# Transposes on halves of 64 rows and a regrouped attention step in a fused attention and mixture-of-experts kernel

## Chip, cores and metric

The kernel runs on one NeuronCore of a Trainium2 chip. The metric is the time of one execution on the device in microseconds (us); the result before is the median of three runs. An engine executes its own queue in order: TensorE (PE, with its weight loads PEld), VectorE (DVE), ScalarE (ACT), GpSimd (POOL); SyncE (SP) issues most DMAs. Engines wait for one another by semaphores.

## What is computed

Local attention (window 64) over 4 x 8 heads of 576 x 64, then a dense two-layer part with ELU, then eight experts weighted by a normalised gate:

```python
scores = scale * np.matmul(q, k.transpose(0, 1, 3, 2))
mask = (rel >= 0) & (rel < window)
scores = np.where(mask, scores, -1000000000.0)
attn = np.exp(scores - np.max(scores, axis=-1, keepdims=True))
attn = attn / (np.sum(attn, axis=-1, keepdims=True) + 1e-09)
x = np.matmul(attn, v)                 # reshaped to (2304, 512)
h = x @ w_in
g = np.where(h > 0.0, h, alpha * (np.exp(np.minimum(h, 0.0)) - 1.0))
x = g @ w_out                          # (2304, 512) -> 2048 -> 512
logits = x @ w_gate                    # gate, normalised 8 times by rows and columns
for e in range(E):
    out += P[:, e:e + 1] * (np.maximum(x @ w1[e], 0.0) @ w2[e])
```

All arithmetic is float32; products are split into high and low parts (three matmuls of 512 columns each take the place of one).

## The kernel before

The program has an attention loop of 27 steps, the rest of the dense part, and the experts. The change concerns the loop alone. It is written as a hand-made order: each engine executes its instructions in the order in which the Python code issues them.

Heads go in 16 pairs (`pair_load`, q and k of two heads). A pair has 9 chunks of 64 positions, taken in 3 groups; a step of the loop handles two groups, that is 6 chunks of two heads, in a software pipeline. In step m the loop issues

- `pair_T`: PE transposes q and k for step m+1 (four transposes of 96 columns for each of two groups, tile `ptr`), and ACT copies them to `qkT`;
- `step_S`: the scores of step m, 12 matmuls on quarters of the array (the trace shows 24, two passes each), tiles `s`; DVE adds the mask and takes the row minimum of the negated scores in six custom instructions (L368), three for each head, into `sp` and `smx`;
- `grp_E`: six exponentials of step m-1 on ACT (L383), and `step_N`: DVE's reciprocal and POOL's multiplication (L399);
- `grp_P`: PE transposes the weights of step m-2 (six transposes of 128 columns, tiles `pt`), and ACT copies them to `pT`;
- `step_V`: P times V of step m-3, tile `pv` (24 matmuls in the trace); `grp_XH` copies it on ACT to `xh`, and `grp_X` subtracts on DVE, giving the low part `xl` (L454);
- up to three slots (`slot`), each for one product of the dense part: six matmuls of 512 columns. An incoming product (`m0_in`, L473 to L475, "i") is half of a bank `p1`; when the second half is done, `elu` issues relu (L238) and exp (L239) on ACT, max (L227) on DVE, a copy to `gh` (L231) on ACT and a subtraction to `gl` (L235) on DVE. An outgoing product ("o", L491 to L493) ends after two with a DVE copy. A budget of 16/6 a step says how many slots are filled. Where a product is not ready, the first steps issue a warm-up matmul (`warm`);
- background work (`run_bg`): conversion of the 64-bit weights by DVE and ACT (L152 to L163), POOL's split of them (L179, L180), and their loads (`w_load`) on SP; `v_load` and `v_shift` bring v and a copy of it shifted by 64 rows (`ve`).

PSUM has four buffers of the pool tagged `ac` (`ps_ac`) for `s`, `ptr`, `pv` and one `pt`, one tagged `sm` for the other `pt`, and three for products. A tag's buffers are handed out in turn, so a new tile waits for the readers of the one issued four requests ago. A step makes six requests of `ac`: before in the order s, s, ptr, ptr, pv, pt.

The order of PE in a step before is scores, one or two products, q/k transposes, P times V, a product, P's transposes. "Step 15" in the text is the step whose scores are the 15th, counted from 0.

Of the kernel before, what the change touches and what calls it, by code (L numbers as in the profile page):

```python
# [8 lines left out]
F32 = mybir.dt.float32  # L9
# [9 lines left out]
def kernel(  # L19
# [88 lines left out]
    def ps_ac(name):  # L108
        return ps.tile([P, 512], F32, tag="ac", bufs=4, name=name)
# [77 lines left out]
    def run_bg(n):  # L187
        for _ in range(min(n, len(bg))):
            bg.pop(0)()
# [61 lines left out]
        return gh, gl  # L251


    NTQ, TQ = 6, S // 6
    qk_nat, v_nat, qk_T = {}, {}, {}

    def pair_load(pi):
        b, hp = divmod(pi, NPAIR)
        h0 = 2 * hp
        t = {}  # L260
        for z, (nm, src) in enumerate((("q", q), ("k", k))):
            if pi % 3 == 2:
                w = NTQ * 2 * D
                x = acc[3][:TQ, z * w:(z + 1) * w].rearrange("p (t h d) -> p t h d", h=2, d=D)
            else:
                x = at.tile([TQ, NTQ, 2, D], F32, tag="nat", bufs=4, name=f"{nm}n")
            for h in range(2):
                (nc.scalar if pi == 0 and z else nc.sync).dma_start(
                    out=x[:, :, h, :],
                    in_=src[b, h0 + h].rearrange("(t p) d -> p t d", p=TQ),  # L270
                )
            t[nm] = x
        qk_nat[pi] = t

    def v_load(pi):
        b, hp = divmod(pi, NPAIR)
# [28 lines left out]
                    0.0, 1.0, op0=ALU.add, op1=ALU.mult,  # L305
                )

    def pair_T(n):
        pi, g = divmod(n, NG)
        if g == 0:  # L310
            qk_T[pi] = at.tile([P, 2, S], F32, tag="qkT", bufs=2, name="qkT")
        pt = ps_ac("ptr")
        per = NTQ // NG
        for m, nm in enumerate("qk"):
            for t in range(per):
                o = (m * per + t) * TQ
# [5 lines left out]
        w = per * TQ  # L322
        nc.scalar.activation(
            qk_T[pi][:, :, g * w:(g + 1) * w],
            pt[:, :2 * w].rearrange("p (m t) -> p m t", m=2), AF.Copy,
        )

    g_st = {}

# [70 lines left out]
                out=sp, in0=sp, in1=w[:, :, h:h + 1].to_broadcast([P, GRP, P]), op=ALU.mult  # L400
            )

    def grp_P(m, h):
        sp = g_st[m, h]
        pt = (ps_ac if h else ps_sm)("pt")
        for l in range(GRP):
            nc.tensor.transpose(pt[:, P * l:P * l + P], sp[:, l, :], ident)
        pT = at.tile([P, GRP * P], F32, tag="pT", bufs=2, name="pT")
        nc.scalar.activation(pT, pt[:, :GRP * P], AF.Copy)
        g_st[m, h] = pT  # L410

    def step_V(m, pv):
        pTs = [g_st.pop((m, h)) for h in range(2)]
        for x in range(2 * GRP):
            pi, c = at_chunk(2 * GRP * m + x)
            ve, vo = v_nat[pi]
            vt, w = (vo, (c - 1) // 2) if c % 2 else (ve, c // 2)
            for h in range(2):
                nc.tensor.matmul(
                    pv[D * h:D * h + D, WIN * x:WIN * x + WIN],  # L420
                    vt[:, w, h, :],
                    pTs[h][:, WIN * x:WIN * x + WIN],
                    start=True,
                    stop=True,
                )
# [824 lines left out]
    with tc.manual_schedule():  # L1250
# [26 lines left out]
                nc.tensor.matmul(pw, wz[:, 0:P], wz, start=True, stop=True)  # L1277

        warm(8)
        for n in range(2):  # L1280
            pair_T(n)
        for kk in range(2 * UF):
            bg += w_tasks(kk)
        NGRP = B * NPAIR * NG
# [31 lines left out]
        for m in range(NST + 3):  # L1316
# [4 lines left out]
            if m == 0:  # L1321
                w_load(0)
                pair_load(2)
                w_load(1)
            if ready():
                budget += 16.0 / per_b
            rate = (0, 0) if m == 0 else (2, 2) if m < 8 else (6, 2)
            mm, mo, mf = m - 1, m - 2, m - 3
            if mid:
                grp_E(mm, 0)  # L1330
            if new:
                step_S(m)
            slot(m, 2)
            run_bg(rate[0])
            if mid:
                grp_E(mm, 1)
            slot(10, 1)
            if mid:
                step_N(mm)
            for n in nxt:  # L1340
                pair_T(n)
            for n in mid if m == 4 else old:
                if n > NG and n % NG == 0 and (n // NG > 2 or m == 4):
                    v_shift(n // NG)
            if fin:
                pv = ps_ac("pv")
                step_V(mf, pv)
                grp_XH(fin, pv)
            slot(m, 0)
            grp_X()  # L1350
            if old:
                grp_P(mo, 0)
                grp_P(mo, 1)
            if fin and (m - 2) % per_b == 0:
                avail += subs[(m - 2) // per_b - 1]
            if m == 13:
                bg += [w_tasks(2 * UF + x)[0] for x in range(2)]
            run_bg(rate[1])
# [7 lines left out]
        grp_X()  # L1366
        avail += subs[4]
        attn_cm.__exit__(None, None, None)
        wb_cm, wb = pool("wb")
# [225 lines left out]
```

## Time and profile before

| | us |
|---|---|
| median of three runs | 1969.49 (1969.34 to 1969.82) |
| profiled execution | 1974.2 |
| its span | 1972.4 |
| PE busy | 1954.1 (99%) |
| DVE busy | 1494.2 (76%) |
| ACT busy | 858.4 (44%) |
| POOL busy | 726.1 (37%) |

The shares are means over the whole span; the attention loop is the first 173 us of it, and there they differ from stage to stage. Matmuls overlap, so what one costs is read from the distance between starts, and a busy PE can still be waiting inside its pipeline. "Idle before" names what ended a wait, as inferred from semaphores.

### The profile page before, as it was taken

Reading aid. Unit: us, or ns where it says so; the run is one execution under the profiler, and the core shown is the slowest. Engines: PE = TensorE matmul, PEld = TensorE weight load, DVE = VectorE, ACT = ScalarE, POOL = GpSimd, SP = SyncE. Lnnn points to the kernel's source line nnn. Section 1 sums busy time; section 2 is a strip of 40 time slices with the busy share of each in tenths; the row PEclk is TensorE's granted clock in tenths of the full one; section 3 lists DMA queues with packets and bytes.
Section 4 is the critical chain, followed back from the end, with each engine's and each line's share of the span. In section 5 each row is a group of like instructions: output and inputs, shape, how many; then the busy total and the mean of one; then the engine's idle time right before and its main releaser. Section 6 shows DMA issues by size and latency. Waiting matters only on the chain.

```text
span 1972.4 us, 33582 instructions
## 1 busy us (share of the span) xinstructions
PE 1954.1 (99%) x11856; PEld 1816.9 (92%) x11856; DVE 1494.2 (76%) x2534; ACT 858.4 (44%) x1801; POOL 726.1 (37%) x723
## 2 busy tenths in 40 slices
PE   8999999999999999999999999999999999999999
PEld 6788888898878888899999999999999999999998
DVE  6746676767698656567787888888888888888886
ACT  8875555555543444333343333333334333333332
POOL 5423232332355554342342323323343323333232
PEclk9999999999999999999999999999999999999999
DMA  9851354467699999868878888888887887888884
GB/s 212 165 110 52 100 173 151 154 210 275 213 381 374 374 366 365 314 234 284 263 242 305 260 261 257 255 266 262 291 260 250 270 266 259 260 260 262 238 279 121
DMA packets 307640, 487.84 MB, mean 247 GB/s; under 512 B 79872, under 2 KB 161936, under 8 KB 303632
## 3 DMA queue, kind: packets, MB, share of 16 engines
q1 hardware_dynamic: 306288, 485.39, 76.3%
q8 instruction: 95, 1.56, 0.3%
q14 instruction: 73, 0.60, 0.1%
q10 hardware_dynamic: 1184, 0.30, 0.1%
HBM read 354.44 MB, written 126.95 MB: 244 GB/s over the span
## 4 chain that ended last, share of the span: by engine, by line
PE 90%; DVE 4%; DMA 2%; ACT 2%; SPq 1%; issue 1%; POOL 0%; ACTq 0%; DVEq 0%; POOLq 0%
PE la L1080 15%; PE ob L1160 11%; PE oa L1160 11%; PE lb L1080 11%; PE p L204 3%; PE ac L538 3%; PE p L206 3%; PE ac L540 3%; PE p L205 2%; PE ac L539 2%; PE ac L904 2%; PE ac L905 2%; PE ac L906 2%; PE p L886 2%; PE p L888 2%; PE p L887 2%
## 5 line engine op out<-in xcount | busy, mean ns | idle before, releaser
L1062 POOL TENSOR_TENSOR h<-s,h 128x384 fp32r<-128x384 f32 x304 | 352.6, 1175 | 721.1 <-ACT h L1053 680.2
L1080 PE MATMUL la<-xf,w1f 128*128 128x384 f32 x1824 | 360.0, 335 | 1.9 <-ACT u L1100 1.3
L1080 PEld LDWEIGHTS la<-xf,w1f 128*128 128x128 f32 x1824 | 318.3, 188 | 3.4 <-ACT u L1100 2.1
L1080 PE MATMUL lb<-xf,w1f 128*128 128x384 f32 x1368 | 273.7, 334 | 0.0
L1053 ACT ACTIVATE h<-s 128x384 fp32r<-128x384 f32 x304 | 155.1, 522 | 245.7 <-DVE s L1104 238.4
L1160 PE MATMUL oa<-h,w2f 128*128 128x384 f32 x1344 | 252.2, 334 | 0.0
L1160 PE MATMUL ob<-h,w2f 128*128 128x384 f32 x1344 | 252.0, 334 | 0.2 <-DVE acc L1177 0.2
L1080 PEld LDWEIGHTS lb<-xf,w1f 128*128 128x128 f32 x1368 | 239.9, 188 | 0.0
L1160 PEld LDWEIGHTS ob<-h,w2f 128*128 128x128 f32 x1344 | 234.4, 188 | 0.5 <-DVE acc L1177 0.5
L1160 PEld LDWEIGHTS oa<-h,w2f 128*128 128x128 f32 x1344 | 234.4, 188 | 0.1
L1058 DVE SCALAR_TENSOR_TENSOR h<-c,h 128x384 fp32r<-128x384 f32 x228 | 187.6, 833 | 31.9 <-ACT h L1053 31.2
L1053 ACT ACTIVATE h<-c 128x384 fp32r<-128x384 f32 x228 | 119.7, 525 | 173.7 <-DVE c L1090 162.6
L725 POOL TENSOR_TENSOR sw<-rw 128x256 f32<-128x256 f32 x110 | 101.0, 919 | 204.6 <-DVE f L755 127.8
L1090 DVE TENSOR_TENSOR c<-c,pb 128x384 f32<-128x384 f32 x192 | 144.5, 753 | 6.6
L1177 DVE TENSOR_TENSOR acc<-oa,acc 128x768 f32<-128x768 f32 (+1 forms) x114 | 105.0, 924 | 37.4 <-PE oa L1160 37.4
L1177 DVE TENSOR_TENSOR acc<-ob,acc 128x768 f32<-128x768 f32 (+1 forms) x110 | 101.2, 923 | 37.1 <-PE ob L1160 37.1
L1104 DVE SCALAR_TENSOR_TENSOR s<-c,s 128x384 f32<-128x384 f32 x152 | 108.3, 713 | 12.0 <-DMA out_dram<-ost 1.0
L246 ACT ACTIVATE hh<-p 128x512 fp32r<-128x512 f32 (+1 forms) x80 | 39.2, 490 | 171.9 <-PE p L888 171.8
L247 DVE SCALAR_TENSOR_TENSOR hl<-p,hh 128x512 fp32r<-128x512 f32 (+1 forms) x80 | 44.3, 556 | 88.5 <-ACT hh L246 88.5
L886 PE MATMUL p<-xh,f 128*128 128x512 f32 (+1 forms) x320 | 108.4, 339 | 0.0
L887 PE MATMUL p<-xl,f 128*128 128x512 f32 (+1 forms) x320 | 107.6, 336 | 0.0
L888 PE MATMUL p<-xh,f 128*128 128x512 f32 (+1 forms) x320 | 107.5, 336 | 0.0
(175 smaller groups left out, 3907.3 us busy)
## 6 DMA issues: line engine op xcount, KB each, us to landing
w1f<-wdi SPq DMA_DIRECT2D x532, 256.0 KB, 4.0
w2f<-wdo SPq DMA_DIRECT2D x266, 512.0 KB, 4.4
wdo<-f SPq DMA_DIRECT2D x28, 1024.0 KB, 7.7
rw<-in_moe_w_dram SPq DMA_DIRECT2D x220, 128.0 KB, 4.9
wdi<-f SPq DMA_DIRECT2D x27, 1024.0 KB, 7.1
wdo<-f SPq DMA_DIRECT2D x28, 768.0 KB, 5.6
wdi<-f SPq DMA_DIRECT2D x27, 768.0 KB, 5.0
raw<-in_moe_w_in_dram SPq DMA_DIRECT2D x16, 512.0 KB, 4.3
```

The lines of the kernel that those rows point to most:

```text
L725: nc.gpsimd.tensor_tensor(out=sw[:, o], in0=a, in1=b, op=op)
L886: nc.tensor.matmul(p1[:, :n], w[:, s, 0, cs], xh, start=(c == 0), stop=False)
L887: nc.tensor.matmul(p1[:, :n], w[:, s, 0, cs], xl, start=False, stop=False)
L888: nc.tensor.matmul(p1[:, :n], w[:, s, 1, cs], xh, start=False, stop=(c == NCC - 1))
L1053: nc.scalar.activation(h[:, 0], src, AF.Relu if relu else AF.Copy)
L1058: nc.vector.scalar_tensor_tensor(h[:, 1], src, 0.0, r(h[:, 0]), op0=ALU.max, op1=ALU.subtract)
L1062: nc.gpsimd.tensor_tensor(out=h[:, 1], in0=src, in1=r(h[:, 0]), op=ALU.subtract)
L1080: nc.tensor.matmul(o, w[:, a, c, :], x[:, b, c, :], start=first and c == 0 and z == 0, stop=last and c == 1 and z == 2, skip_group_check=True,
L1090: nc.vector.tensor_tensor(out=t, in0=t, in1=pb[g, e][:, i], op=ALU.mult)
L1104: nc.vector.scalar_tensor_tensor(d[nm], d[a], 0.0, d[b], op0=ALU.max, op1=op)
L1160: nc.tensor.matmul(o[:, c], w[:, p, b, c * P:(c + 1) * P], hs[p][:, a, :], start=fresh and p == 0 and z == 0, stop=False, skip_group_check ...
L1177: nc.vector.tensor_tensor(out=a, in0=src, in1=a, op=ALU.add)
```

## The change

Two things change. First, transposes: q and k of a pair now lie in one tile of 128 rows (q in rows 0 to 63, k in rows 64 to 127, nine chunks of 64), and both q/k and P are transposed in halves of 64 rows, which alternate between two PSUM tiles; the two tiles are then copied to SBUF by ACT, one for q (or the upper half) and one for k (or the lower half). Second, the order of a step: P times V of step m-3 with its copies, scores, exponentials, P's transposes, q/k transposes, `v_shift`, conversions, normalisation, and then all slots. A step's requests of `ac` now come as pv, s, s, pt, ptr, ptr. Products of a block can begin in the step whose P times V completes it, since that now stands ahead of the slots.

```diff
-    def pair_T(n):
...
-                nc.tensor.transpose(
-                    pt[:, o:o + TQ],
-                    qk_nat[pi][nm][:, g * per + t].rearrange("p h d -> p (h d)"),
-                    ident[:TQ, :TQ],
-                )
...
+    def step_T(ns):
+        pts = [ps_ac("ptr") for _ in range(2)]
...
+            for b in range(GRP):
+                for z, zs in enumerate(halves):
+                    nc.tensor.transpose(
+                        pts[z][:, o + b * WIN:o + b * WIN + WIN],
+                        qk_nat[pi][zs, g * GRP + b].rearrange("p h d -> p (h d)"),
+                        ident[zs, zs],
+                    )
...
+        for pi, t0, o, w in segs:
+            for z in range(2):
+                nc.scalar.activation(qk_T[pi][:, z, t0:t0 + w], pts[z][:, o:o + w], AF.Copy)
...
-    def grp_P(m, h):
...
-        for l in range(GRP):
-            nc.tensor.transpose(pt[:, P * l:P * l + P], sp[:, l, :], ident)
...
+    def step_P(m):
+        pts = [ps_sm("pt"), ps_ac("pt")]
+        for h in range(2):
+            for l in range(GRP):
+                o = (GRP * h + l) * WIN
+                for z, zs in enumerate(halves):
+                    nc.tensor.transpose(pts[z][:, o:o + WIN], g_st[m, h][zs, l, :], ident[zs, zs])
...
-            if mid:
-                grp_E(mm, 0)
-            if new:
-                step_S(m)
-            slot(m, 2)
-            run_bg(rate[0])
-            if mid:
-                grp_E(mm, 1)
-            slot(10, 1)
-            if mid:
-                step_N(mm)
-            for n in nxt:
-                pair_T(n)
...
             if fin:
                 pv = ps_ac("pv")
                 step_V(mf, pv)
                 grp_XH(fin, pv)
+                grp_X()
+                if (m - 2) % per_b == 0:
+                    avail += subs[(m - 2) // per_b - 1]
+            if ready():
+                budget += 16.0 / per_b
+            if new:
+                step_S(m)
+            if mid:
+                grp_E(mm, 0)
+                grp_E(mm, 1)
+            if old:
+                step_P(mo)
+            if nxt:
+                step_T(nxt)
...
+            run_bg(rate[0])
+            if mid:
+                step_N(mm)
+            slot(m, 2)
+            slot(10, 1)
             slot(m, 0)
-            grp_X()
-            if old:
-                grp_P(mo, 0)
-                grp_P(mo, 1)
-            if fin and (m - 2) % per_b == 0:
-                avail += subs[(m - 2) // per_b - 1]
```

On PE, before, around the scores of step 18 (`p_1976` is a bank of incoming products, `[waits ...]` the engines whose semaphores an instruction waits for):

```order
L473 MATMUL p_1976<-xh_94,w0h 128x512
L474 MATMUL p_1976<-xl_99,w0h 128x512
L475 MATMUL p_1976<-xh_94,w0l 128x512
L407 MATMUL pt<-ident,sp 128x128 [waits Pool_49]
L407 MATMUL pt<-ident,sp 128x128 x2
L407 MATMUL pt<-ident,sp 128x128 [waits DVE_49,PE_49,Pool_49]
L407 MATMUL pt<-ident,sp 128x128 x2
L354 MATMUL s<-qkT 64x128 [waits Activation_49] x2
L354 MATMUL s<-qkT 64x128 x10
L473 MATMUL p_1976<-xh_94,w0h 128x512
L474 MATMUL p_1976<-xl_99,w0h 128x512
L475 MATMUL p_1976<-xh_94,w0l 128x512
```

The same engine now, at a step with outgoing products (`p_1796`), from the last of P times V to the first product:

```order
L424 MATMUL pv<-pT,ve 64x64 x2
L354 MATMUL s<-qkT 64x128 [waits DVE_49,Activation_49]
L354 MATMUL s<-qkT 64x128 [waits PE_49]
L354 MATMUL s<-qkT 64x128 x10
L409 MATMUL pt<-ident,sp 128x64 [waits Pool_49]
L409 MATMUL pt<-ident,sp 128x64 [waits PE_49]
L409 MATMUL pt<-ident,sp 128x64 x4
L409 MATMUL pt<-ident,sp 128x64 [waits Pool_49]
L409 MATMUL pt<-ident,sp 128x64 x5
L315 MATMUL ptr<-ident,qkn 128x64 [waits DMAHW3_49,DMAHW4_49,DVE_49,PE_49]
L315 MATMUL ptr<-ident,qkn 128x64 [waits DMAHW5_49,DMAHW6_49,DVE_49,PE_49]
L315 MATMUL ptr<-ident,qkn 128x64 x10
```

Scores, P's and q/k transposes now follow each other with no product between, and the first transpose of either half of q/k waits for DVE.

On ACT, before, with the ELU of an incoming product (`p_1819`), two copies of q/k, the copies `xh`, two `pT` and six exponentials:

```order
L238 ACTIVATE m<-p_1819 128x512
L239 ACTIVATE m<-m 128x512
L323 ACTIVATE qkT<-ptr 128x2x192 x2
L447 ACTIVATE xh_96<-pv 128x192
L447 ACTIVATE xh_95<-pv 128x192
L231 ACTIVATE gh<-m 128x512
L409 ACTIVATE pT<-pt 128x384 x2
L383 ACTIVATE sp,smx<-sp,smx 128x128 x6
```

ACT now, at the like place:

```order
L326 ACTIVATE qkT<-ptr 128x384 x2
L238 ACTIVATE m<-p_2031 128x512
L239 ACTIVATE m<-m 128x512
L231 ACTIVATE gh<-m 128x512
L452 ACTIVATE xh_95<-pv 128x192
L452 ACTIVATE xh_96<-pv 128x192
L383 ACTIVATE sp,smx<-sp,smx 128x128 x6
L412 ACTIVATE pT<-pt 128x384 x2
```

The copies of q/k moved ahead of relu and exp; `gh` stands directly behind exp, and `xh` behind `gh`.

## Rows read from the trace of the kernel before

**Rows 1.** Windows: busy us of each engine (instructions), granted clock, DMA.

```profile
20.00:42.00 22.00, 19.87 (x287) 15.76 (x287) 17.44 (x82) 21.41 (x85) 12.78 (x18) 0.93 1.05 225
42.02:93.99 51.97, 47.76 (x525) 38.22 (x525) 37.51 (x147) 43.63 (x151) 25.65 (x30) 0.96 0.79 161
93.99:136.76 42.77, 42.77 (x469) 34.58 (x468) 23.21 (x110) 34.54 (x121) 11.95 (x18) 1.00 0.67 146
```

**Rows 2.** Timeline of PE, steps 16 and 17: start us, us, operation.

```profile
105.29 0.82 PE L317 MATMUL ptr<-ident,acc 96*128 96x96 f32 x8
106.04 0.34 PE L419 MATMUL pv<-pT,ve 128*64 128x64 f32 x4
...
106.68 0.29 PE L419 MATMUL pv<-pT,ve 128*64 128x64 f32 x4
106.89 0.50 PE L473 MATMUL p<-xh,w0h 128*128 128x512 f32 x1
107.23 0.40 PE L474 MATMUL p<-xl,w0h 128*128 128x512 f32 x1
...
108.42 0.82 PE L407 MATMUL pt<-ident,sp 128*128 128x128 f32 x6
109.16 0.89 PE L354 MATMUL s<-qkT 64*64 64x128 f32 x24
109.98 0.50 PE L473 MATMUL p<-xh,w0h 128*128 128x512 f32 x1
```

**Rows 3.** Lines L317 and L407: weight loads, ns min/median/max.

```profile
L317 PEld LDWEIGHTS ptr<-ident,qn x66: 137/140/143, 5.4 to 148.4; 96*128 96x128 f32 x66
...
L407 PEld LDWEIGHTS pt<-ident,sp x144: 138/140/230, 15.9 to 168.9; 128*128 128x128 f32 x144
```

**Rows 4.** Timeline of ACT in the same step.

```profile
103.58 0.38 ACT L383 ACTIVATE sp<-sp,smx 128x128 f32<-128x128 f32 x1
...
105.89 0.57 ACT L238 ACTIVATE m<-p 128x512 f32<-128x512 f32 x1
106.50 0.63 ACT L239 ACTIVATE m<-m 128x512 f32<-128x512 f32 x1
107.03 0.86 ACT L323 ACTIVATE qkT<-ptr 128x384 f32<-128x384 f32 x2
107.78 0.56 ACT L447 ACTIVATE xh<-pv 128x192 fp32r<-128x192 f32 x2
108.20 0.65 ACT L231 ACTIVATE gh<-m 128x512 fp32r<-128x512 f32 x1
108.94 0.87 ACT L409 ACTIVATE pT<-pt 128x384 f32<-128x384 f32 x2
```

**Rows 5.** Timeline of DVE in the same step.

```profile
103.39 0.28 DVE L368 CUSTOM_DVE_ANT_0 sp<-s,mask 128x128 f32<-128x128 f32 x1
...
104.02 0.28 DVE L368 CUSTOM_DVE_ANT_0 sp<-s,mask 128x128 f32<-128x128 f32 x1
...
104.66 0.69 DVE L235 TENSOR_TENSOR gl<-m,gh 128x512 fp32r<-128x512 f32 x1
107.16 0.69 DVE L227 SCALAR_TENSOR_TENSOR m<-m,p 128x512 f32<-128x512 f32 x1 [1.82 <-ACT m L239]
...
108.37 0.62 DVE L454 TENSOR_TENSOR xl<-pv,xh 128x192 fp32r<-128x192 f32 x2 [0.22 <-ACT xh L447]
```

**Rows 6.** Groups by line, first 260 us: one of ACT's two weight conversions.

```profile
L158 ACT ACTIVATE raw<-raw 128x512 int32<-128x512 uint32 x21 | 14.2, 678 | 0.2 <-DMA raw<-in_moe_w_in_dram 0.2
```

**Rows 7.** Timeline of PE: two rows with an idle gap before them.

```profile
51.26 0.34 PE L419 MATMUL pv<-pT,ve 128*64 128x64 f32 x4 [1.21 <-DMA ve<-vo]
...
83.44 0.48 PE L419 MATMUL pv<-pT,ve 128*64 128x64 f32 x4 [1.68 <-POOL sp L399]
```

**Rows 8.** Windows around the two gaps.

```profile
51.00:57.00 6.00, 5.63 (x67) 4.55 (x68) 3.84 (x12) 4.56 (x13) 4.03 (x5) 1.00 1.20 236
81.00:88.00 7.00, 5.32 (x48) 4.18 (x49) 2.30 (x8) 1.84 (x6) 1.61 (x2) 0.76 0.79 156
```

More of the change, by code (lines that the diff above doesn't have):

```diff
@@ L251, in relu @@
         return gh, gl
-    NTQ, TQ = 6, S // 6
+    halves = [slice(0, WIN), slice(WIN, P)]
     qk_nat, v_nat, qk_T = {}, {}, {}
@@ L259, in pair_load @@
         h0 = 2 * hp
[L260 to L266, printed above, removed]
+        if pi % 3 == 2:
+            x = acc[3][:, 0:NCH * P].rearrange("p (t h d) -> p t h d", h=2, d=D)
+        else:
+            x = at.tile([P, NCH, 2, D], F32, tag="nat", bufs=2, name="qkn")
+        for z, src in enumerate((q, k)):
             for h in range(2):
                 (nc.scalar if pi == 0 and z else nc.sync).dma_start(
-                    out=x[:, :, h, :],
-                    in_=src[b, h0 + h].rearrange("(t p) d -> p t d", p=TQ),
-                )
-            t[nm] = x
-        qk_nat[pi] = t
+                    out=x[halves[z], :, h, :],
+                    in_=src[b, h0 + h].rearrange("(t p) d -> p t d", p=WIN),
+                )
+        qk_nat[pi] = x
     def v_load(pi):
@@ L306, in v_shift @@
                 )
-    def pair_T(n):
[L309 to L316, printed above, removed]
-                nc.tensor.transpose(
-                    pt[:, o:o + TQ],
-                    qk_nat[pi][nm][:, g * per + t].rearrange("p h d -> p (h d)"),
-                    ident[:TQ, :TQ],
-                )
[L322 to L326, printed above, removed]
+    def step_T(ns):
+        pts = [ps_ac("ptr") for _ in range(2)]
+        segs = []
+        for i, n in enumerate(ns):
+            pi, g = divmod(n, NG)
+            if g == 0:
+                qk_T[pi] = at.tile([P, 2, S], F32, tag="qkT", bufs=2, name="qkT")
+            o = i * GRP * WIN
+            for b in range(GRP):
[5 more added lines that the diff above has]
+                    )
+            if segs and segs[-1][0] == pi:
+                segs[-1][3] += GRP * WIN
+            else:
+                segs.append([pi, g * GRP * WIN, o, GRP * WIN])
+        for pi, t0, o, w in segs:
+            for z in range(2):
+                nc.scalar.activation(qk_T[pi][:, z, t0:t0 + w], pts[z][:, o:o + w], AF.Copy)
     g_st = {}
@@ L1279 @@
         warm(8)
-        for n in range(2):
-            pair_T(n)
+        step_T([0, 1])
         for kk in range(2 * UF):
@@ L1348 @@
                 grp_XH(fin, pv)
-            slot(m, 0)
-            grp_X()
-            if old:
-                grp_P(mo, 0)
-                grp_P(mo, 1)
-            if fin and (m - 2) % per_b == 0:
-                avail += subs[(m - 2) // per_b - 1]
+                grp_X()
[12 more added lines that the diff above has]
+                step_T(nxt)
+            for n in mid if m == 4 else old:
+                if n > NG and n % NG == 0 and (n // NG > 2 or m == 4):
+                    v_shift(n // NG)
+            run_bg(rate[0])
[3 more added lines that the diff above has]
+            slot(10, 1)
+            slot(m, 0)
             if m == 13:
@@ L1365 @@
                     pair_load(pi)
-        grp_X()
         avail += subs[4]
```

21 lines of the change are left out of this document (8 added, 13 removed).

## The prediction

> **What bounds the kernel now.** I read the windows first, by stage, then PE's own rows of one step, then ACT's and DVE's of the same step, and last PE's idle gaps. The change touches only the attention loop, which fills the first 173 of 1972 us; everything behind it is the same program, and there PE is busy nearly throughout. Inside the loop there are three regimes [rows 1]. From 20 to 42 us ACT is busy 21.41 of 22 us: ACT sets the pace, PE fills gaps with warm products. From 42.02 to 93.99 (steps 8 to 14, counted by their scores) ACT is busy 43.63 of 51.97 us and PE has gaps. From 93.99 to 136.76 PE is busy 42.77 of 42.77 us: six steps (15 to 20) with 16 expert products, nothing waits. So in this last regime PE's own work sets the time, and only there can cheaper PE work be a gain.
>
> The price of a step on PE comes from the starts in [rows 2]: q/k transposes 0.75 us (105.29 to 106.04), P times V 0.85, one product of six matmuls 1.53 alone (106.89 to 108.42; its first matmul takes 0.34, the others 0.24), so 1.42 when it follows another product, P's transposes 0.74, scores 0.82. Attention is 3.16 us a step; six steps with 16 products in 12 bursts make 6 x 3.16 + 16 x 1.42 + 12 x 0.11 = 43.0, and the window says 42.77: the prices hold.
>
> **The change part by part.** *The transposes.* P's six of 128 columns become twelve of 64, the eight of 96 for q and k become twelve of 64; row halves alternate between two PSUM banks. No row shows such a half. The scores run four quarter-array products side by side, 24 in 0.82 us or 34 ns each; that is the lower bound: 12 x 0.034 = 0.41. The upper one is the pace of the present q/k transposes, 94 ns each: 1.13. I take 0.5 for each group, near the scores' row, since those too sit on 64-row halves: 0.49 us a step less work for PE, with bounds of 0.67 less and 0.77 more.
>
> The weight loads of 96 and of 128 rows take the same 140 ns [rows 3], and there are now 24 in a step for 14. [...]
>
> *Merged products.* Two bursts a step become one: 0.11 us less in each of some 17 steps.
>
> *The order.* This is what decides. Before, q/k transposes stood one or two products behind the scores, and P times V behind those. Now the PE row is V, S, P, T, then all products. The four buffers of the pool named ac go round; T's first bank is the one that P times V wrote in the same step, its second the one that the scores' first head wrote. So T waits on DVE for xl (L459 of the new program) and for the first three masked reduces (L368), and the products queue behind T. What must pass: P times V is seen done 0.93 us after it starts (106.68 + 0.29 - 106.04), then ACT's xh 0.42, DVE's xl 0.62 and three reduces 0.63 [rows 2, 4, 5]; with a hand-over of some 0.05 each, T's second half starts 1.8 us after xh and T ends 2.4 us after it. From V's start that is 3.35 us, against 3.16 now: what the halves save, the wait takes back, and the merged burst returns 0.11. A step whose ACT and DVE are idle at its start is thus +0.1: three outgoing products 2.4 + 4.37 + 0.95 = 7.7 (now 7.6), two 6.3 (now 6.2).
>
> Steps that finish an incoming product (i) are worse, because ACT's xh now stands behind the whole ELU: relu 0.61, exp 0.53, DVE's max 0.69, ACT's copy gh 0.65 [rows 4, 5], 2.55 us with hand-overs. Before, exponentials and copies of the attention were queued between exp and gh, and covered DVE's max; now ACT stands there and waits. ACT's fixed row in a step is xh 0.42, six exponentials 2.31, pT 0.87, qkT 0.75: 4.35 us, then relu. Counting from xh to the next xh, products starting at 2.4:
> - two outgoing, one finishing i at the end: i ready at 2.4 + 4.37 + 0.15 = 6.9, plus 2.55: 9.45
> - three i, the second finishes: 5.5 + 2.55 = 8.05
> - two i, the first finishes: ACT free at 4.35, plus 2.55: 6.9
> - one i and two o: 7.7; three o 7.7; two o 6.3.
>
> Steps 15 to 20 are just these six: 46.1 against 42.77, +3.3; DVE's gl (0.69) also stands ahead of xl where xh is late, longer than xh itself by 0.27, in three steps: +0.8. So **+4.1** there. Steps 21 and 22 repeat the first two (+2.8), the last four have no T and gain 1.0 on P's transposes and bursts: **+1.8**.
>
> Steps 8 to 14: products begin at the end of step 8, one step sooner than now, but step 12 gets none (the output weights are not converted yet), so both hold 15 by step 14. Chain: 8.5, 9.2, 8.1, 8.1 for steps 8 to 11, which are the same cases with two conversions of 0.68 on ACT [rows 6], paced at some 1.2 us together and partly inside the wait for max; 4.35 for the empty step; 7.7 and 6.3: 52.2 against 51.97, **+0.3**. That stretch is not clean before either: PE waits 1.21 us for ve's DMA and 1.68 us at 83.44 [rows 7].
>
> The first eight steps stay with ACT. Its work is the same but for four qkT copies in place of two in every third step, and xh must now wait for a P times V that itself waits for pT: some 0.2 us a step: **+1**. The loads are the same in bytes; SP and POOL now get v_shift ahead of the conversions, so ve's copies no longer queue behind a weight load that waits for DVE. That can only help.
>
> *The clock.* [...] T's wait is 0.6 us in a clean step and 0.6 to 2.3 us in the ten steps that finish an i. [...]
>
> Sum: 1 + 0.3 + 4.1 + 1.8 + 3 = +10.2 us. The profiled execution took 1974.2 us (span 1972.4), 4.7 more than the median of 1969.49; the difference is carried to the median: **1980 us**.
>
> **The rivals.** *Faster: the holes of steps 8 to 14 close.* Seven steps with 15 products in 12 bursts at PE's own price are 7 x 3.16 + 15 x 1.42 + 12 x 0.11 = 44.7 us; they take 51.97, so 7.3 us are gaps and slow clock. Two products now fall into step 8, where PE idles before the scores, and ve comes sooner. If ACT keeps its xh ahead of PE (it decides whether xh starts within 1 us of V's start), the 7.3 go and the later blocks break even: 1962. For it: the gaps at 51.26 and 83.44; against: ACT is 84% busy there [rows 1, 7].
>
> *No change.* Half of those 7.3 us come back, ACT's early pace holds and the clock does not fall: 10.2 - 0.3 - 3.65 - 1 - 3 leaves +2.2, 1972. For it: the same gaps; against: three things must go well together.
>
> *Slower still: the loads are not shared.* If each half pays a load as the present transposes do, T takes 1.13 in place of 0.5; P's delay vanishes in T's wait, T's does not: 0.63 x 14 steps (8 to 22 without 12) = +8.8: 1989. For it: the equal loads [rows 3]; against: the scores' 34 ns. [...]
>
> **How the numbers follow.** Forecast 0.50 (1974 to 1986), faster 0.20 (1962), no change 0.17 (1972), slower still 0.13 (1989). Faster or slower means by over 0.2%, 4 us, about what a measurement here can tell from none: 0.20, 0.17, 0.63. The range goes from 1962, the middle of the faster case, to 1993, the end of the last: it leaves out about 0.1 below and less above.
>
> **What would show it.** In the profile after: PE idle in front of L315, released by DVE's xl or smx, 0.6 us in steps with outgoing products and over 1 us where an i ended; ACT idle in front of gh (L231) by DVE's m; twelve halves in about 0.5 us; scores 46 us apart from step 15 to 21; step 12 without a product. I am wrong if PE never waits at L315, if xl and reduces are done before P's transposes end, or if steps 8 to 14 take under 48 us.

## The result and the profile after

The changed kernel takes 1997.27 us (median of four runs, 1996.32 to 1998.72) against 1969.65 for the kernel before on the same chip: a ratio of 1.0133, 95% interval 1.0121 to 1.0146, so it is 27.6 us **slower**. The forecast said slower, but 1980, and its range ended at 1993. In the profiled executions the spans are 1996.0 and 1972.4 us; all of that difference lies in the attention loop, which now ends at some 197 us instead of 173.

The same three stages as in [rows 1], in the changed kernel (step 0 to 7 end with the scores at 47.97 us, steps 8 to 14 at 107.00, steps 15 to 20 at 157.86; the columns are busy us of PE, weight loads, DVE, ACT, POOL with instruction counts, then granted clock, DMA share, GB/s):

```profile
20.00:47.97 27.97, 21.33 (x393) 15.99 (x393) 18.30 (x91) 24.94 (x102) 15.83 (x22) 0.94 1.16 208
47.97:107.00 59.03, 49.78 (x599) 38.42 (x595) 36.47 (x142) 44.57 (x155) 23.81 (x29) 0.88 0.69 136
107.00:157.86 50.86, 44.32 (x533) 34.61 (x529) 24.58 (x114) 33.87 (x123) 12.71 (x19) 0.93 0.66 127
```

The stage in which PE was busy 42.77 of 42.77 us now takes 50.86 with PE idle for 6.5 of them; the stage ahead of it went from 51.97 to 59.03. The granted clock fell from 0.96 and 1.00 to 0.88 and 0.93. Against before, the first eight steps lost 5.95 us, the next seven 7.06, the six after them 8.09, and the rest 2.5.

Step 16, the step of [rows 2, 4, 5], in time order on PE, DVE and ACT:

```profile
117.86 0.89 PE L354 MATMUL s<-qkT 64*64 64x128 f32 x24
118.41 0.69 DVE L227 SCALAR_TENSOR_TENSOR m<-m,p 128x512 f32<-128x512 f32 x1 [3.92 <-ACT m L239]
118.67 0.58 PE L409 MATMUL pt<-ident,sp 64*128 64x64 f32 x12
119.13 0.63 ACT L231 ACTIVATE gh<-m 128x512 fp32r<-128x512 f32 x1 [0.76 <-DVE m L227]
119.67 0.53 ACT L452 ACTIVATE xh<-pv 128x192 fp32r<-128x192 f32 x2
120.23 0.62 DVE L459 TENSOR_TENSOR xl<-pv,xh 128x192 fp32r<-128x192 f32 x2 [1.14 <-ACT xh L452]
120.77 0.28 DVE L368 CUSTOM_DVE_ANT_0 sp<-s,mask 128x128 f32<-128x128 f32 x1
...
121.00 0.24 PE L315 MATMUL ptr<-ident,acc 64*128 64x64 f32 x1 [1.74 <-DVE xl L459]
...
121.63 0.87 PE L315 MATMUL ptr<-ident,acc 64*128 64x64 f32 x11 [0.38 <-DVE smx L368]
...
122.43 0.79 PE L478 MATMUL p<-xh,w0h 128*128 128x512 f32 x1
```

This is the queue that the forecast described: ACT idles 0.76 us for DVE's max, copies gh, and only then xh; xl follows; PE sits 1.74 us in front of the first transpose of q and k and 0.38 us in front of the second, with three products behind it.

What the forecast didn't have stands one step earlier, in step 15 (DVE, POOL and PE):

```profile
105.71 0.69 DVE L162 CUSTOM_DVE_ANT_0 t<-raw,t 128x1024 uint16<-128x1024 uint16 x1 [2.46 <-ACT raw L158]
...
107.64 0.19 DVE L396 RECIPROCAL smx<-smx 128x6 f32<-128x6 f32 x1
107.98 2.06 POOL L399 TENSOR_TENSOR sp<-sp,smx 128x384 f32<-128x384 f32 x2 [12.12 <-ACT sp L383]
108.86 0.40 PE L409 MATMUL pt<-ident,sp 64*128 64x64 f32 x6 [0.98 <-POOL sp L399]
110.10 0.40 PE L409 MATMUL pt<-ident,sp 64*128 64x64 f32 x6 [0.83 <-POOL sp L399]
```

DVE waits 2.46 us in a background conversion for ACT; the normalisation is queued behind it, POOL multiplies late, and P's transposes, which now follow the scores directly, wait 1.8 us for POOL.

(The view names ACT as POOL's releaser; DVE's reciprocal ended at 107.83, just before POOL began.) Step 15 has a second bound. The next P times V, at 117.01, reads a copy of v that stands on SP's queue behind a weight load and loads of q and k: its two transfers were issued at 110.8 and 111.8 and took 5.4 and 5.0 us to land, so they came by 116.8. Without P's wait PE would soon have waited for that copy.

And behind both waits the clock falls. Windows through steps 15 and 16, as in [rows 8]:

```profile
107.00:110.28 3.28, 1.47 (x40) 1.09 (x37) 3.25 (x12) 2.79 (x13) 2.21 (x3) 1.00 0.50 137
110.28:114.80 4.52, 4.48 (x27) 3.52 (x26) 2.93 (x13) 2.31 (x7) 0.70 (x1) 0.62 1.29 201
...
117.86:121.60 3.74, 1.64 (x41) 1.22 (x37) 2.06 (x10) 2.98 (x12) 0.00 (x0) 1.00 1.34 175
121.60:125.00 3.40, 3.37 (x17) 2.80 (x18) 1.44 (x9) 2.41 (x10) 1.91 (x3) 0.51 1.10 186
```

After PE was busy for 1.47 of 3.28 and 1.64 of 3.74 us, the next 4.52 and 3.40 us ran at a granted clock of 0.62 and 0.51. A product's matmuls start 0.43 us apart there (123.02 to 124.73), and 0.23 us apart at 1.00 (115.06 to 116.68). PE was busy in nearly all of that time (4.48 and 3.37 us), so an estimated 1.7 us of its work were lost in each (0.38 of 4.52 and 0.49 of 3.40 us). The deepest dip is step 13, behind step 12, which has no product (PE busy 3.51 of 5.98 us). First step 13 of the changed kernel, then of the one that has the new order with whole transposes:

```profile
90.50:100.67 10.17, 10.17 (x94) 7.95 (x91) 4.71 (x21) 4.42 (x19) 3.40 (x6) 0.66 1.00 181
```

```profile
83.56:92.61 9.05, 7.56 (x83) 6.00 (x81) 4.71 (x21) 4.53 (x19) 4.61 (x6) 1.00 0.88 216
```

The second runs at 1.00 and is still only 1.1 us shorter, because PE, busy 7.56 of 9.05 us, waits there: here lost clock is not all lost time.

What PE waited for, from 8 to 200 us (us in total, times, longest us):

```profile
PE ptr L315 <- DVE xl L459: 6.5, 5, 1.7
PE ptr L315 <- DVE smx L368: 6.3, 16, 0.4
PE pt L409 <- POOL sp L399: 4.7, 9, 1.0
PE pv L424 <- DMA ve<-vo: 3.2, 3, 2.0
PE pv L424 <- ACT pT L412: 1.7, 3, 0.8
```

### The profile page after: what moved, and what is told of

Read it like the earlier page. It is cut to its first block, busy times and chain, and to the rows that moved or that the text cites. A ratio compares the mean times of both kernels' runs of the same rounds, so it can differ in the third digit from the quotient of the medians.

```text
span 1996.0 us, 34079 instructions
## 1 busy us (share of the span) xinstructions
PE 1956.9 (98%) x12096; PEld 1814.2 (91%) x12096; DVE 1496.4 (75%) x2534; ACT 859.0 (43%) x1817; POOL 728.9 (37%) x723
## 4 chain that ended last, share of the span: by engine, by line
PE 89%; ACT 4%; DVE 3%; DMA 2%; SPq 1%; POOL 1%; issue 1%; POOLq 0%; ACTq 0%; DVEq 0%
PE la L1085 15%; PE ob L1165 11%; PE lb L1085 11%; PE oa L1165 11%; PE p L205 2%; PE ac L544 2%; PE p L204 2%; PE ac L543 2%; PE p L206 2%; PE ac L545 2%; PE p L891 2%; PE p L892 2%; PE p L893 2%; PE ac L909 2%; PE ac L910 2%; PE ac L911 2%
## 5 line engine op out<-in xcount | busy, mean ns | idle before, releaser
L730 POOL TENSOR_TENSOR sw<-rw 128x256 f32<-128x256 f32 x110 | 105.0, 955 | 201.2 <-DVE f L760 108.2
```

The lines of the kernel that those rows point to most:

```text
L730: nc.gpsimd.tensor_tensor(out=sw[:, o], in0=a, in1=b, op=op)
```

## The experiments

Four theories. **A**: T, the transposes of q and k, waits for xl and the reduces, worse where ACT does the ELU first. **B**: P's transposes wait for POOL, because the normalisation stands behind conversions, or because P comes too early. **C**: the first steps pay for loading q and k onto 64 rows each. **D**: the waits cost twice, once by their length and once by the lower clock behind them. V is P times V. The table is read from the starts of the scores and from the granted clock of the first 200 us of each profiled execution. Medians of the kernel before were 1969.65 to 1970.42 us in the six sets of runs; its profiled execution was 1974.2, 4.6 above, so differences of the stages to before are too small by up to that. Each row of stages is one execution: the changed kernel and the runs with warm products and with gh behind xh issue the same instructions up to step 8, and reach it at 47.97, 48.99 and 49.53, so differences of under some 1.6 us in that column mean little.

| kernel | median us | scores 8 at | steps 8–14 | steps 15–20 | step 16 | clock |
|---|---|---|---|---|---|---|
| before | 1969.65 | 42.02 | 51.97 | 42.77 | 7.58 | 0.97 |
| changed | 1997.27 | 47.97 | 59.03 | 50.86 | 10.94 | 0.91 |
| halves, old order | 1973.81 | 46.23 | 49.72 | 41.14 | 7.23 | 0.97 |
| new order, whole transposes | 1984.82 | 43.82 | 54.97 | 48.63 | 9.22 | 0.98 |
| P's halves, old order | 1967.78 | 41.20 | 49.05 | 41.56 | 7.38 | 0.99 |
| P's halves, new order | 1986.61 | 44.64 | 58.69 | 48.51 | 9.22 | 0.95 |
| changed, T behind all products | 1985.26 | 48.28 | 54.86 | 44.60 | 7.84 | 0.95 |
| changed, T behind two slots | 1983.09 | 48.54 | 55.05 | 44.36 | 7.35 | 0.92 |
| changed, gh behind xh | 1989.01 | 49.53 | 54.85 | 47.92 | 8.19 | 0.93 |
| changed, normalisation first | 1995.97 | 50.41 | 58.83 | 47.20 | 7.74 | 0.91 |
| changed, warm products | 1993.75 | 48.99 | 56.56 | 51.61 | 9.40 | 0.95 |
| changed, P behind two slots | 1990.87 | 49.67 | 54.25 | 46.58 | 8.70 | 0.97 |
| changed, T and P there | 1986.31 | 51.13 | 55.17 | 43.04 | 7.44 | 0.91 |
| the same, q and k in 96 rows | 1981.76 | 46.15 | 53.12 | 43.86 | 7.48 | 0.97 |
| the same, V there too | 1969.93 | 40.53 | 49.61 | 41.52 | 7.37 | 0.99 |

### The two parts alone

Halves without the order: the loop of the kernel before, with

```diff
-            for n in nxt:
-                pair_T(n)
+            if nxt:
+                step_T(nxt)
...
-                grp_P(mo, 0)
-                grp_P(mo, 1)
+                step_P(mo)
```

> The half transposes alone, with the new loads of q and k, in the order of the kernel before. If the order is what costs, this is no slower than before: twelve halves take about 0.55 us in place of 0.75, twice a step, which in steps 15 to 20 (PE busy throughout) is some 0.4 us a step, so 2 to 4 us less: 1965 to 1968 us. If the halves themselves cost (their weight loads, four copies in place of two where a pair ends, two banks held until ACT has copied both), it is above 1975.

Measured 1973.81, ratio 1.0020 (1.0011 to 1.0029): 3.6 us slower, not faster. Steps 15 to 20 gained what was expected (three outgoing products 7.23 in place of 7.58 us), but the first eight steps lost it: scores 8 at 46.23 in place of 42.02.

The order without halves: the loop of the changed kernel with the old `pair_T`, `grp_P`, loads and P times V.

> The new order alone, with the transposes, loads and banks of the kernel before. If the order is what costs, it is at or above the changed kernel, 1995 to 2003 us, since each transposing group also takes 0.2 us more of PE. If the halves are what costs, it lies near before, under 1978.

Measured 1984.82, ratio 1.0071 (1.0056 to 1.0087). It fits neither forecast: the order costs 14.6 us and the halves 3.6, together 18, and the change costs 27.6. The missing 9 are an interaction. Some 6.3 of them lie in steps 10, 13, 16 and 22, which take 7.74, 9.05, 9.22 and 9.22 us with whole transposes, all at a clock of 1.00, and 9.50, 10.17, 10.94 and 10.94 in the changed kernel, at 0.82, 0.66, 0.84 and 0.84. So it goes with the clock (0.98 against 0.91 in the first 200 us); why the clock falls in one and not in the other was not tested.

### Where halves cost: q and k in the first steps

P's halves alone, q and k in 96 rows, first in the old order, then in the new (its edit against the changed kernel is shown, cut to the main lines):

```diff
-        x = at.tile([P, NCH, 2, D], F32, tag="nat", bufs=2, name="qkn")
+        x = at.tile([TQ, NTQ, 2, D], F32, tag="nat", bufs=4, name=f"{nm}n")
...
-                step_T(nxt)
+                pair_T(n)
```

> The kernel before with the halves for P alone; q and k are loaded and transposed in 96 rows as before, and the order is the old one. If the loss of the first eight steps in the run with both kinds of halves (first scores at 8.38 in place of 6.95 us, step 8 at 46.2 in place of 42.0) comes from loading q and k onto 64 rows each, step 8 is again at 42 to 42.6 us, steps 15 to 20 take 0.15 to 0.2 us less each than 7.6, and the time is 1966 to 1969 us. If P's halves slow the first steps, it is 1972 or more.

Measured 1967.78, ratio 0.9987 (0.9978 to 0.9996): as expected, and 2.3 us **under the kernel before**. Scores 8 start at 41.20, 5.0 us sooner than with both kinds of halves. The transfers of the first 40 us, q and k onto 64 rows (halves, old order) and then in 96 rows (P's halves, old order):

```profile
DMA packets 22618, 7.51 MB, mean 188 GB/s; under 512 B 20437, under 2 KB 22485, under 8 KB 22613
```

```profile
DMA packets 24035, 8.60 MB, mean 215 GB/s; under 512 B 21601, under 2 KB 23649, under 8 KB 24030
```

With 64 rows less is moved in the same time, in a stretch where the transfer engines are busy: the DMA share is 1.15 up to 20 us and 1.08 from there to 46.23 us with 64 rows, and 1.08 up to 41.20 us with 96. About half of the 1.09 MB between the two is one weight load of 512 KB that the faster kernel issues within the 40 us; nearer to the point, the loads of q and k onto 64 rows took 5.4 and 5.6 us from issue to landing (medians), those in 96 rows 4.8 and 5.0. This pair of runs also differs in T's copies, so the share of the loads by themselves was not measured.

> The changed kernel with q and k loaded and transposed in 96 rows as before; the new order and P's halves stay. If the loads of q and k onto 64 rows and the two shared banks of their transposes are what the halves cost in this order, step 8 is at 43.5 to 44.5 us in place of 47.97, and the time 1982 to 1988 us. If P's halves are what costs there (V waits for both copies), it stays above 1992.

Measured 1986.61, as expected: 10.7 us under the changed kernel by undoing only q's and k's half. Scores 8 came at 44.64, just past the 44.5 expected. So q's and k's halves do cost in the first steps, as theory C says; whether by their loads or by T's extra copies on ACT, the busy engine there (24.94 of 27.97 us from 20 us on in the changed kernel), is not shown. The 3.4 us between 44.64 and 41.20 are the order's part of the first steps.

### T's wait

T moved behind all products, then behind the second of the three slots:

```diff
-            if nxt:
-                step_T(nxt)
...
             slot(10, 1)
+            if nxt:
+                step_T(nxt)
             slot(m, 0)
```

> The changed kernel with the transposes of q and k behind all products of the step, where xl and the reduces are long done. Theory A: the waits at L315 for DVE (about 13 us) go, products start right behind P, and with the clock that stays up the time falls by 10 to 18 us, to 1979 to 1987. Theory B: only P's wait counts, so the time stays above 1992. A risk to both: the copies of the transposes come late and the next step's scores wait for them.

Measured 1985.26. The waits at T fell to 1.3 us, and the risk came true; PE from 8 us on:

```profile
PE s L354 <- ACT qkT L326: 11.4, 11, 2.2
PE pt L409 <- POOL sp L399: 4.1, 10, 0.8
```

> The changed kernel with the transposes of q and k behind the second of the three product slots: xl and the reduces are done by then, and a product covers the copies that the next scores need. Theory A: PE waits neither at L315 for DVE (13 us) nor, as with the transposes last, at the scores for the copies (11.4 us); the time falls to 1976 to 1983 us. Theory B: it stays above 1990.

Measured 1983.09, 14.2 us under the changed kernel, the largest gain of any single move, and 0.1 above the upper end of what was expected. Neither T nor the scores wait much; step 16 takes 7.35 us, as the halves do in the old order. What stays is P:

```profile
PE pt L409 <- POOL sp L399: 6.8, 14, 0.8
PE s L354 <- ACT qkT L326: 2.5, 4, 0.9
```

### ELU ahead of xh

The copy gh that is left over at a step's end goes behind the next xh:

```diff
                 grp_XH(fin, pv)
+            run_later()
+            if fin:
                 grp_X()
...
             run_bg(rate[1])
-            run_later()
```

> The changed kernel with ACT's copy gh, where it is left over at a step's end, written behind the next step's xh. The forecast took ELU's chain of 2.55 us ahead of xh as the price of the steps that finish an incoming product. Theory A: xh comes 1.3 us sooner in such steps, xl with it, PE waits at L315 under 0.5 us there in place of 1.7, the clock does not fall behind it, steps 16 and 22 take about 9.3 in place of 10.94 us, and the whole falls by 4 to 9 us, to 1988 to 1993. If the delay comes back in the outgoing products, which need gh, steps 16 and 22 stay above 10 us.

Measured 1989.01, 8.3 us less. Steps 16 and 22 take 8.19 and 8.18 us in place of 10.94. Step 16, on ACT and PE:

```profile
115.06 0.89 PE L354 MATMUL s<-qkT 64*64 64x128 f32 x24
115.49 0.53 ACT L452 ACTIVATE xh<-pv 128x192 fp32r<-128x192 f32 x2
...
116.34 0.63 ACT L231 ACTIVATE gh<-m 128x512 fp32r<-128x512 f32 x1 [0.32 <-DVE m L227]
...
116.98 0.24 PE L315 MATMUL ptr<-ident,acc 64*128 64x64 f32 x1 [0.51 <-DVE xl L459]
```

xh starts 0.43 us after the scores in place of 1.81: 1.4 us sooner, with 1.3 expected. T waits 0.51 instead of 1.74, and the clock is 1.00 in this step where it was 0.84. So of the 2.75 us that the step gained, 1.2 is the wait, and the rest is about the clock's loss (0.16 of 10.94 us is 1.75).

### The clock

Three warm products, whose result nothing uses, between P and T from step 8 on:

```diff
+            if m >= 8 and nxt:
+                warm(3)
             if nxt:
                 step_T(nxt)
```

> The changed kernel with three warm products (no result is used) between P's transposes and those of q and k, from step 8 on, some 0.7 us of PE where it otherwise waits for xl. Theory D (the waits cost mainly by the clock that falls behind them): steps 16 and 22, which took 10.94 us each with some 3.4 us at the lower clock, take about 9.3, the clock of the first 200 us rises, and the time falls by 4 to 9 us, to 1988 to 1993. If the waits cost by their own length alone, the time stays or rises by up to 4 us, since the warm products also run where no wait is.

Measured 1993.75, 3.5 us less, just short of the expected 4. Step 16 as a window, changed kernel and then this one:

```profile
117.86:128.80 10.94, 8.81 (x94) 6.93 (x91) 4.18 (x19) 6.71 (x23) 2.01 (x3) 0.84 1.09 165
```

```profile
118.33:127.73 9.40, 8.17 (x98) 6.25 (x94) 4.18 (x19) 6.71 (x23) 2.02 (x3) 1.00 1.19 175
```

The step still waits for xl (0.84 and 0.38 us) and does 0.7 us more work on PE, yet ends 1.54 us sooner, with a clock of 1.00 in place of 0.84. Steps 16 and 22 alone are 3.1 us. Where no wait is, the warm products cost their time (steps 18 to 20 together 0.4 us more), and step 15, whose wait at P they don't cover, became longer. Theory D is shown for the dips behind T in steps 16 and 22 (0.84 in both in the changed kernel, 1.00 here).

### The normalisation

Normalisation ahead of the step's background conversions:

```diff
-            run_bg(rate[0])
             if mid:
                 step_N(mm)
+            run_bg(rate[0])
```

> The changed kernel with the normalisation (DVE's sum and reciprocal, POOL's products) written ahead of the background conversions of the step. Theory B (P's transposes wait for POOL because the normalisation stands behind conversions that wait for ACT): PE's 12.7 us of waits at L409 for POOL shrink to under 4 and the time falls by 6 to 14 us, to 1983 to 1991. Theory A (the wait of q's and k's transposes for xl and the reduces is what costs): those waits remain, P's delay goes into them, and the time stays within 4 us of 1997.

Measured 1995.97, no change to speak of. P's waits for POOL went from 4.7 to 1.4 us, and T's for xl from 6.5 to 6.8. (The 12.7 us of the expectation add to PE's 4.7 the 8.0 of its weight loads, which wait at the same time.) That looked like theory A's answer, though P's delay did not go into T's waits: steps 15 to 20 fell by 3.7 us, and step 8 came 2.4 later. So it was repeated with T behind two slots:

> The transposes of q and k behind the second product slot (1983.1 us alone), and the normalisation ahead of the background conversions besides. With T out of the way, theory B can show: P's waits for POOL at L409 (6.8 us) fall under 3, step 15 takes about 8.5 in place of 10.65 us, and the time is 1974 to 1980 us. If conversions that come later then hold up the first weights, steps 8 to 13 lengthen and the time stays within 3 us of 1983.

Measured 1990.30: 7 us *slower* than without it, and step 15 still 10.79 us. PE's waits from 0 to 200 us:

```profile
PE pv L424 <- DMA ve<-vo: 6.0, 2, 3.3
PE s L354 <- ACT qkT L326: 5.7, 3, 4.2
...
PE pt L409 <- POOL sp L399: 0.9, 4, 0.3
```

P no longer waits, but V waits 3.27 us in step 15 for a copy of v whose transfer stands on SP's queue behind a weight load and the loads of q and k:

```profile
109.50 0.37 SPq L133 DMA_DIRECT2D raw<-in_moe_w_in_dram  x1
109.97 1.34 SPq L266 DMA_DIRECT2D qkn<-in_q_dram  x2
111.36 1.80 SPq L266 DMA_DIRECT2D qkn<-in_k_dram  x2
113.27 1.38 SPq L297 DMA_DIRECT2D ve<-vo  x2
```

The copy is issued 4.17 us after the step's scores, against 3.65 with T alone moved, so it is only 0.5 us later; PE, which no longer waits at P, comes to V 2.85 us sooner (6.95 us after the scores in place of 9.80) and waits for it. In step 15 of this version the copy of v, not the normalisation, sets the length. Theory B in the form "the normalisation stands too late" falls there; in the rest of the loop scores 8 come 2.6 us later and steps 8 to 14 take 58.01 us in place of 55.05, and what part of that the later conversions have was not tested. Adding gh behind xh to that version:

> As the run before it, and gh behind xh besides. With T behind two products nothing on PE waits for xl within a step, so by theory A the ELU's place is worth nothing here any more: within 3 us of that run. If xh behind the ELU still holds up the next V or the copies of P, it gains 3 to 6 us.

Measured 1989.91, no different, as expected: with T behind two products, xh's place costs nothing that shows.

### P, then T and P, then V, out of the chain

P's transposes alone behind the second slot (`step_P(mo)` after `slot(10, 1)`):

> The changed kernel with P's transposes behind the second product slot; those of q and k stay right behind the scores. Theory B as slack (P right behind the scores comes before POOL has normalised): P's waits at L409 for POOL (12.7 us with those of the loads) go, step 15 takes about 8.5 in place of 10.86 us, and the time falls by 4 to 10 us, to 1987 to 1993. Theory A: P's 0.58 us only covered part of the wait for xl, which grows by as much; the time stays within 3 us of 1997.

Measured 1990.87, 6.4 us less. P waits 0.3 us for POOL, step 15 takes 9.28 in place of 10.86, and the clock of the first 200 us is 0.97; T and V wait more:

```profile
PE ptr L315 <- DVE xl L459: 10.5, 11, 2.1
PE pv L424 <- ACT pT L412: 7.7, 8, 1.7
...
PE pt L409 <- POOL sp L399: 0.3, 1, 0.3
```

So P directly behind the scores costs, but not by its wait alone: PE's waits at T for xl and at V grew by 4.0 and 6.0 us, more than the 4.4 that P's fell by. What rose is the clock, from 0.91 to 0.97. Theory B's other form, that P comes too early, is supported and not shown apart from the clock. Then both behind the second slot, T ahead of P, and after that the same with q and k in 96 rows:

> The changed kernel with both transposing groups behind the second product slot. If the two places of PE in front of unfinished work of other engines (xl for T, POOL for P) are what the order costs from step 8 on, steps 15 to 20 take as long as with the halves in the old order (41.1 us in place of 50.9), step 15 included, and the time is 1975 to 1980 us; with T alone moved it was 1983.1. If step 15 stays near 10.7 us, it is held by something else, and the time stays at 1981 or more.

Measured 1986.31, a miss: 3.2 us more than with T alone moved. Step 15 fell to 8.49, steps 15 to 20 to 43.04, but the step-8 scores come at 51.13 in place of 48.54, and now V, first in the step, follows P too closely:

```profile
PE pv L424 <- ACT pT L412: 9.0, 11, 1.3
PE pv L424 <- POOL sp L399: 3.0, 1, 3.0
```

> As the run before it, with q and k loaded and transposed in 96 rows as in the kernel before. If the loads onto 64 rows cost their 4 to 5 us in the first eight steps and nothing else, it is 4 to 5 us under that run and within 4 us of the kernel before: 1969 to 1974 us. If putting V and the scores first costs by itself, it stays above 1976.

Measured 1981.76: 4.5 us less than the run before it, and scores 8 5.0 us sooner. q and k in halves cost what was expected; but it is 12 us from the kernel before, so what stands first in the step costs as well. One more run moves V with xh and xl between T and P. On PE that is the old order again, but for P, which stands in front of the step's last product in place of behind it:

> As the run with T and P behind the second product slot and q and k in 96 rows (1981.8 us), and P times V with xh and xl also put there, between T and P; scores and exponentials still come first, the normalisation stays where the changed kernel has it. If V at the start of the step, right behind the copies of P, is the rest of the loss (PE's waits at V for pT, POOL and DVE are 10.6 us there), these go and the time comes to within 4 us of P's halves in the old order: 1966 to 1972 us. If the place of the exponentials and of the normalisation, which this run keeps, costs as well, it stays above 1975.

Measured 1969.93, ratio 0.9998 (0.9989 to 1.0008): all 12 us are gone. The exponentials behind the scores, and the normalisation behind the conversions, are kept here and cost nothing that can be measured against before. Against P's halves in the old order the profile is level up to the last scores (146.41 and 146.57 us) and loses 2.1 us behind them, where PE waits once for gl, 2.0 us, which the other kernel does not. PE's longest waits in it, from 8 us on:

```profile
PE s L355 <- ACT qkT L324: 5.7, 7, 1.6
PE p L498 <- DVE gl L235: 2.0, 1, 2.0
```

### A better version

P's halves in the old order beat both kernels. One try for more takes q and k in halves from pair 8 on, whose loads the loop issues in step 8, behind the first steps:

> The old order, P's halves throughout, and q and k in halves only from pair 8 on, when the loads of the first steps are past (pairs 0 to 7 in 96 rows, as before). If the loads onto 64 rows cost only while the transfers set the pace, the first eight steps are as with P's halves alone (step 8 at 41 to 42 us), steps 15 to 20 take 7.23 in place of 7.38 us where three products run, and the time is 0.5 to 2 us under that run's 1967.8: 1965.8 to 1967.5.

Measured 1968.02, ratio 0.9988 (0.9979 to 0.9997). The steps are as expected (scores 8 at 40.98, steps 15 to 20 40.68 in place of 41.56), but the median is not under that of P's halves alone; its runs spread from 1966.3 to 1972.4, and the two can't be told apart.

## Why the forecast was right in sign and wrong in size

**The halves' price: right.** Twelve were taken at 0.5 us. In the old order with P's halves twelve start at 104.50 and the scores behind them at 105.01:

```profile
104.50 0.59 PE L410 MATMUL pt<-ident,sp 64*128 64x64 f32 x12
105.01 0.34 PE L355 MATMUL s<-qkT 64*64 64x128 f32 x4
```

That is 0.51, or 43 ns each, though a load of 64 rows still takes 138 ns (changed kernel), as long as those of [rows 3]:

```profile
L409 PEld LDWEIGHTS pt<-ident,sp x288: 134/138/226, 17.6 to 188.2; 64*128 64x128 f32 x144
```

So the rival "the loads are not shared" is excluded. The time of a load did not fall with its rows (138 ns with 64 rows, 140 with 96 and with 128), but the loads of the halves lie beside one another and beside the matmuls: in step 16 of the changed kernel twelve of them, 12 x 0.138 = 1.66 us one by one, keep PEld busy for 0.45 us from 118.67 on, where the twelve transposes start. That decides here. Step 12 without a product came as forecast, too.

**T's wait and the ELU chain: right as a mechanism, and near in size where the clock stayed up.** Steps 17 to 20 were given 6.9, 7.7, 7.7 and 6.3 and took 6.83, 8.14, 7.74 and 6.35. Steps 15 to 17 were given 9.45 + 8.05 + 6.9 = 24.4 and took 28.63; less the 1.72 (4.52 us at 0.62) and 1.67 (3.40 us at 0.51) lost to the clock that leaves 25.2. That is what the forecast has with its 0.8 for gl ahead of xl, but by luck: in the trace xl starts 0.2 us late by gl in steps 17 and 18 and nowhere else in these six, and step 15 holds P's wait and the copy of v, which the forecast did not price. The run with gh behind xh shows the mechanism by itself.

**P and V: the failed step of the order.** The forecast followed T's producers and put P's wait for POOL at nothing, without a reason. Between the normalisation and the P that uses it, the old order had the rest of a step and then the scores, q/k transposes, V and products of the next; the new one has the step's products, V and the scores, and P waited for POOL nine times, 4.7 us. Moving P alone gained 6.4 us, clock included. For V's wait on the copies of P it took 0.2 us a step in the early stage alone; moving V was worth 11.8 us once T and P were out of the way. And "ve's copies no longer queue behind a weight load that waits for DVE" was wrong in step 15: SP's queue waited 9.9 us for DVE in front of the weight load at 107.22, and the copies came 3.6 us behind it. In the run with the normalisation first and T moved, V waits for such a copy.

**The first eight steps: +1 forecast, +5.95 measured.** The forecast gave q's and k's halves nothing here but the extra copies, since "The loads are the same in bytes"; they cost 3.3 us in the changed kernel's own order (47.97 against 44.64) and 5.0 in two others (46.23 against 41.20, and 51.13 against 46.15). The rest, 2.6 us (44.64 against 42.02), is the order with P's halves. With 1.6 us between like programs at this place, these are sizes and no more.

**The clock: +3 forecast, with the first steps the largest miss.** From step 8 to 20, 0.12 of 59.03 and 0.07 of 50.86 us were lost, 10.6 us, against 2.1 (0.04 of 51.97) before: 8.5 more, at most, since some of it falls on waits, and the last steps add step 22 with its 10.94. The forecast's 3 us were the author's estimate, and no run shows that term. What the runs showed in its place: in step 16 the dip comes behind the wait, when the queued products run (0.51 over 3.40 us, PE busy for 3.37 of them), and with the warm products steps 16 and 22 run at 1.00 and are 3.1 us shorter together, as much as the forecast had for the whole loop.

**Steps 8 to 14: +0.3 forecast, +7.06 measured.** The 52.2 us were built from the rows of steps 16 and 17, whose stage had a clock of 1.00; 59.03 less 7.1 is 51.9, while before's 51.97 holds 2.1 of its own loss. That the two agree so well is luck: not all lost clock lies on the path (with whole transposes this stage takes 54.97 at 0.97), and step by step the forecast is off both ways, 8.5 and 9.2 for steps 8 and 9 that took 7.10 and 11.15.

**Carrying the difference to the median: 4 us.** The profiles differ by 23.6 us, the medians by 27.6, since the profiled execution of before was 4.6 above its own median and that of the changed kernel 0.5. The forecast named the 4.7 but gave no bound for it. One profiled execution can't say where they were lost; step 13, with its gap of 1.68 us [rows 7], takes 11.12 us there and under 7.8 with P's halves in the old order and in the last of the moved versions. That this is the place is likely, not shown.

Together: 5 for the first steps, 11 for steps 8 to 20 less the 3 counted as clock, 0.7 at the end and 4 for the median are 17.4, and the forecast missed by 17.3. **The faster rival** failed by its own test: xh starts 0.97 us after V in step 15 but 2.66 in step 16, behind an ELU (117.01 to 119.67), and 1.3 even with gh behind it, and there steps 8 to 14 still took 54.85.

What stays open: why the order with whole transposes loses little clock and with halves much (the waits for xl are of similar length, 1.35 and 1.60 us in step 10, and with P's halves alone it loses some too, 0.95), and how much of the slower first steps are transfers and how much the copies.

## What to carry to other kernels

When work is regrouped, follow every producer of every moved step back to its queue, and count what stood between producer and consumer before: here each of T, P and V did better with a product or two of other work in between, and the saved instructions, 0.35 us a step (7.58 to 7.23), were no match for what those waits and the lower clock took. A PE wait in front of queued work is priced twice where the clock falls behind it, as in step 16 (1.74 us of wait, then 3.40 us at 0.51), because the lower clock meets the work that was held up. Try each half of a change alone: one of them (P's halves in the old order) was the gain.

## What the hardware showed

Gap length alone did not tell whether the clock fell. In step 10 the changed kernel waited 1.60 and 0.39 us at T, and the step's rest ran at 0.74; with gh behind xh the same step waited 1.64 and 0.39 us, and its rest ran at 1.00. With the normalisation first and T moved, even V's wait of 3.27 us (PE busy 1.63 of 4.90 us) lies in a stretch, 110 to 130 us, that ran at 1.00 throughout. First step 10 of the changed kernel, then of the one with gh behind xh:

```profile
69.23:75.72 6.49, 6.11 (x48) 4.65 (x49) 4.68 (x19) 4.63 (x15) 3.88 (x5) 0.74 0.50 136
```

```profile
70.35:75.28 4.93, 4.54 (x49) 3.51 (x49) 4.69 (x19) 4.14 (x15) 2.31 (x3) 1.00 0.27 88
```

In the old order the loads of q and k onto 64 rows took 5.4 to 5.6 us from issue to landing in the first 40 us where those in 96 rows took 4.8 to 5.0 (medians), with the same 144 KB in each transfer; all transfers together moved 188 and 215 GB/s, a figure that also holds one weight load more in the second. The two versions are 5 us apart by step 8, in a stage in which ACT, not PE, is the busy engine (from 20 us on 23.41 of 26.23 us against PE's 20.82, and 21.20 of 21.20 against 18.54).
